# Reciprocal denominators spread by DMA in float32 in place of products with a selector

## The chip, the cores and the metric

The kernel runs on one core of a Trainium2 chip. The metric is the device time of one execution in microseconds; the figure of a kernel is the median of its runs. The core has a tensor engine (PE, whose weight loads are shown as PEld), VectorE (DVE), ScalarE (ACT), GpSimd (POOL) and SyncE (SP), which here issues every DMA. Each engine works through its own list of instructions in order; semaphores tie the lists together.

## The reference

Linear attention with a feature map is followed by a gated layer with a convolution over three tokens. Eight batches, eight heads, 576 tokens, head dimension 64, 128 features; the layer goes from 512 to 1024 and back. Cut to what is computed:

```python
proj = einsum('bhsd,df->bhsf', x, w_phi)           # x is q, then k
proj = proj - max(abs(proj), axis=-1)
phi = concatenate([exp(proj), exp(-proj)], axis=-1)   # 256 features

kv  = einsum('bhsf,bhsd->bhfd', k_p, v)
z   = sum(k_p, axis=2)
num = einsum('bhsf,bhfd->bhsd', q_p, kv)
den = einsum('bhsf,bhf->bhs', q_p, z)[..., None] + 1e-06
x   = num / den                                     # [B, S, 512], the heads side by side

h    = maximum(x @ w_in, 0)
conv = sum over k of conv_w[k] * h shifted by k - 1 tokens
out  = (h * sigmoid(conv)) @ w_out
```

The part that the change touches is the division. Each token of each head has one denominator, and 64 numerators have to be divided by it.

## The kernel before, in words

**Tiling.** Heads are handled in pairs, and two pairs make a quad; a batch has two quads, so four pairs (p = 0 to 3). The 64 dimensions of the first head of a pair lie on partitions 0 to 63 and those of the second on 64 to 127. A quad's tokens come in five groups. `k_process` loads a group of k and v, projects it and adds to kv; `q_process` loads a group of q, projects it, transposes, takes the exponentials and multiplies with kv. The value matrix has a 65th column of ones, so row 64 of the product `nm` is the denominator, and rows 0 to 63 are the numerators.

**Precision.** Many products work on float32 values split into a rounded part and an exact rest (`split`, L57 to L65), three products for one: with rounded weights and the rounded part, with rounded weights and the rest, with the weights' rest and the rounded part.

**From the products to x.** At the end of `q_process`, ScalarE copies the denominators of a group out of row 64 (L374, tile `dr`), and a DMA (L377) brings them into the tile `den`, 72 partitions by 16 elements. ScalarE copies the numerators of both heads into `num`, 128 partitions by 576 tokens (L379). When a pair is complete, `x_process` runs for it. VectorE adds 1e-6 (L392), takes the reciprocal (L393) and splits it into two parts (L396, recorded at the helper's lines L64 and L65). Four DMAs (L399) lay the parts out in `rr`, four rows (part, head) of 576 tokens. Then, for each half c of 290 tokens, a product with the constant selector `sel_r` (four rows by 128 columns of zeros and ones) sums the two parts and spreads them over the head's 64 partitions (L407, PSUM tile `rb`); VectorE multiplies numerators and `rb` (L409, tile `xf`), and `split` gives `xh` (ScalarE) and `xl` (VectorE), on which the MoE layer's first products work.

**The MoE layer.** `h_part` multiplies `xh` and `xl` of the four pairs with w_in (L432) for a chunk of 288 tokens and one on each side that has one; `conv_process` does the convolution, the sigmoid and the gate; `o_part` multiplies with w_out (L491). There are 16 chunks, two per batch.

**Buffers.** PSUM tiles with the tag "g" share four buffers: the projections of q and k, the transposes, `nm`, and `rb`. `xf` has two buffers, `rr` one, `den` three, `num` four, `xh` and `xl` eight each, which is one batch's worth. A batch's `xh` of half c can thus only be written when the previous batch's products with that half are done.

**The order of work.** The parts are generators. A loop at the end merges them: each yields how long the tensor engine is held ("pe"), how long its next operands take ("wait"), or a condition ("until"). Attention is started ahead of MoE by a rule on what is left of each (`ATT_PE`, `MOE_PE`), and gets a lead in priority (`AHEAD`). A tile framework then orders each engine's instructions by priority and by planned times; the parts of `x_process` that touch the division are traced with high priority. What results is a fixed order for each engine; an instruction whose operand is late holds back all that stand behind it on its engine.

Of the kernel before, what the change touches and what calls it, by code (L numbers as in the profile page):

```python
# [18 lines left out]
P = 128  # L19
NQ = 2            # quads (four heads each) per batch  # L20
TC = 288          # tokens per MoE chunk
HW = TC + 2       # tokens of h computed per MoE chunk (one token of halo, even width)
VW = D + 1
NH = 11           # tiles of h
# the order of work
WINDOW = 13       # chains of attention in flight
LAT = 1.7         # latencies stretched by
TAIL_US = 24      # of the MoE's products, what is left when attention's are done
AHEAD = 300       # instructions by which attention goes before the MoE that it was merged with
# quads whose products are in float32, as long as the tensor engine has time, so that nothing has to be split  # L30
NQ_F32 = 2        # q's projections
NKV_F32 = 2       # the products with kv
# [3 lines left out]
def kernel(  # L36
    ctx: ExitStack,
    tc: tile.TileContext,
    qT: bass.AP,     # [B, NQ, 128 = (i, d), 2*S], the last 64 tokens of either pair in the middle
    kT: bass.AP,     # likewise  # L40
    vt: bass.AP,     # [B, NQ, 128, 20*65]
    wbd: bass.AP,    # [128, 256] block diagonal of w_phi
    w_in: bass.AP,   # [8 = (4 c, 2 halves), 128, 512], in float64 twice as many words
    conv_w: bass.AP,  # [128, (8, 3)], likewise
    w_out: bass.AP,  # [8, 128, DM], likewise
    ident: bass.AP,  # [128, 128]
    selr: bass.AP,   # [4, 128]
    out: bass.AP,    # [B, 4, 128, S]
# [8 lines left out]
    def split(src, hi, lo, eng_hi, eng_lo):  # L57
        """hi: src rounded to 12 significant bits, lo: the exact rest."""
        if eng_hi is nc.scalar:
            nc.scalar.activation(out=hi, in_=src, func=AF.Copy)  # L60
        elif eng_hi is nc.gpsimd:
            nc.gpsimd.tensor_scalar(out=hi, in0=src, scalar1=1.0, scalar2=0.0, op0=ALU.mult, op1=ALU.add)  # L62
        else:
            nc.vector.tensor_copy(out=hi, in_=src)  # L64
        eng_lo.tensor_tensor(out=lo, in0=src, in1=hi.bitcast(F32), op=ALU.subtract)  # L65

# [13 lines left out]
    selr_f = sb.tile([4, P], F32, name="selr_f", tag="qr", bufs=2)  # L80
    nc.sync.dma_start(out=selr_f, in_=selr)
    sel_r = cp.tile([4, P], F32R, name="sel_r")
    nc.vector.tensor_copy(out=sel_r, in_=selr_f)

    # Weights that come as float64 arrive as raw 64-bit words, of a high half (sign, 11 bits
    # of exponent, 20 of fraction) and a low half (32 of fraction). The engines build
    #   power = +-2^e   and   w = (1.fraction) * power, rounded to float32 once.
    # Exponents below float32's give zero, those above it infinity or NaN.
# [18 lines left out]
    def weight_split(src, n, hi, lo):  # L107
        """src: [128, 512] weights in DRAM (float32, or the words of float64)."""
        name = f"w{n}_"
        if src.dtype == F32:  # L110
            raw = sb.tile([P, 512], F32, name=f"{name}r", tag="gh", bufs=2)
            nc.sync.dma_start(out=raw, in_=src)
            split(raw, hi, lo, nc.gpsimd, nc.gpsimd)
            return
        raw = sb.tile([P, 1024], I32, name=f"{name}r", tag="gh", bufs=2)
        nc.sync.dma_start(out=raw, in_=src)
        tmp = sb.tile([P, 2, 512], F32, name=f"{name}t", tag="gl", bufs=2)
        w = tmp[:, 0, :]
        float64_round(raw, w, tmp[:, 1, :])
        split(w, hi, lo, nc.scalar, nc.gpsimd)  # L120
# [24 lines left out]
    # The parts below are processes: generators that trace some instructions and then  # L145
    # yield how long the tensor engine is held by them (pe), how long it is until the
    # next part has its operands (wait), or a condition that has to hold (until). The
    # loop at the end merges them into one order in which products of one process
    # cover the latencies of the others.
# [3 lines left out]
    def pe(ns):  # L153
        return ("pe", ns)
# [11 lines left out]
    # A quad is two pairs of heads. Its tokens come in groups: group 0 is the last 64  # L166
    # tokens of both pairs, groups 1 to 4 are 256 tokens of a pair. A tile of 128 tokens
    # holds a pair of heads, one above the other, against block diagonal weights.
# [16 lines left out]
    def project(n, hi, lo, b, qd, g, kind):  # L185
        """The projection of n tiles of two heads less its greatest magnitude per token and head."""
        if b == 0 and kind == "k":
            # the MoE doesn't use its banks yet
            ps = pm.tile([P, n * 256], F32, name=f"{kind}p{b}_{qd}_{g}", tag="m")
        else:  # L190
            ps = pg.tile([P, n * 256], F32, name=f"{kind}p{b}_{qd}_{g}", tag="g", bufs=4)
# [17 lines left out]
    def after(ins, trace):  # L209
        """Trace an instruction that its engine issues behind ins."""  # L210
        if ins is None:
            return trace()
        with tc.issue_after(ins.ins):
            return trace()
# [5 lines left out]
    def k_process(b, qd, g):  # L220
# [39 lines left out]
        if j < 5:  # L260
            for _ in products():
                pass
            yield pe(860 * n)
        else:
            # five groups later in the order than the queries with whose products these alternate:
            # the loads of either's weights hide behind the other's products
            kvgen[j] = products()
            set_ready(("ke", j))
            yield until(("kvd", j))
        if g == 4:  # L270
            # these take the place of the same quad's of the batch before
# [28 lines left out]
    def q_process(b, qd, g):  # L300
# [15 lines left out]
        # in the order (head, tile) the tokens of a head lie side by side  # L316
# [16 lines left out]
        # pairs of heads in this group, each with its tokens' place in the tile and in the sequence  # L333
# [33 lines left out]
        for pr_, o, s0, w in parts:  # L367
            if (b, qd, pr_) not in den:
# [3 lines left out]
            # denominators in the order (16 tokens, head)  # L372
# [3 lines left out]
                                 func=AF.Copy)  # L376
# [7 lines left out]
    def x_process(b, p):  # L384
# [5 lines left out]
        with tc.high_priority():  # L390
            rc = sb.tile([72, 16], F32, name=f"rc{b}_{p}", tag="rc", bufs=2)
            nc.vector.tensor_scalar(out=dn, in0=dn, scalar1=1e-6, scalar2=None, op0=ALU.add)  # L392
            nc.vector.reciprocal(out=rc, in_=dn)  # L393
            rr = sb.tile([4, S], F32R, name=f"rr{b}_{p}", tag="rr", bufs=1)
            rhl = [sb.tile([72, 16], F32R, name=f"rc{j}{b}_{p}", tag=f"rc{j}", bufs=2) for j in range(2)]
            split(rc, rhl[0], rhl[1], nc.vector, nc.vector)  # L396
            for j in range(2):
                for i in range(2):
                    nc.sync.dma_start(out=rr[2 * j + i : 2 * j + i + 1, :].bitcast(F32).rearrange("o (r c) -> o r c", c=16),  # L399
                                      in_=rhl[j].bitcast(F32).rearrange("(r i) c -> i r c", i=2)[i])  # L400
        yield ("wait", 4500)
        for c in range(2):
            yield until(("h", 2 * (b - 1) + c) if b > 0 else None)
            t0 = 0 if c == 0 else S - HW
            with tc.high_priority():
                rb = pg.tile([P, HW], F32, name=f"rb{b}_{p}_{c}", tag="g", bufs=4)
                nc.tensor.matmul(out=rb, lhsT=sel_r, rhs=rr[:, t0 : t0 + HW], start=True, stop=True)  # L407
                xf = sb.tile([P, HW], F32, name=f"xf{b}_{p}_{c}", tag="xf", bufs=2)
                nc.vector.tensor_tensor(out=xf, in0=nt[:, t0 : t0 + HW], in1=rb, op=ALU.mult)  # L409
                xh[b, p, c] = sb.tile([P, HW], F32R, name=f"xh{b}_{p}_{c}", tag="xh", bufs=8)  # L410
                xl[b, p, c] = sb.tile([P, HW], F32R, name=f"xl{b}_{p}_{c}", tag="xl", bufs=8)
                split(xf, xh[b, p, c], xl[b, p, c], nc.scalar, nc.vector)
            set_ready(("x", b, p, c), 2500)
            yield pe(125)

# [28 lines left out]
    def conv_process(n):  # L444
        c = n % 2
        o = 0 if c == 0 else HW - TC
        for f in range(8):
# [6 lines left out]
            # the tap beyond the batch's first and last token falls on nothing  # L454
# [67 lines left out]
    active = []    # [time, process, is a chain, lead in priority], attention's chains and what they spawn  # L522
# [6 lines left out]
    ATT_PE = B * (18 * 330 + 72 * 215 + 18 * 550 + 8 * 6 * 270 + 4 * 250)  # L529
# [6 lines left out]
    def step(p, kind):  # L536
        """Run process p up to its next pause; False when it ended."""
# [23 lines left out]
    while moe is not None or chains or active:  # L561
        while chains and sum(1 for p in active if p[2]) < WINDOW:
            b, x, g, kind = chains.pop(0)
            # the first batch's attention goes before all else
# [22 lines left out]
        else:  # L587
            # nothing is ready: on to the next time at which something is
# [57 lines left out]
```

## Time and profile before

| | |
|---|---|
| median of three runs | 849.68 us (848.51 to 853.46) |
| the profiled execution, first to last instruction | 848.8 us |
| mean granted clock of the tensor engine | 0.981 |
| instructions | 18003 |
| busy: PE, VectorE, ScalarE, GpSimd | 96%, 73%, 67%, 36% |
| products with the selector (L407) | 64 |
| DMAs from `rc` to `rr` (L399) | 128, of 2.2 KB each |
| mean DMA traffic | 58 GB/s |

The profiled execution's span leaves out what lies before its first and after its last instruction; the median is 0.9 us longer. Matmuls are pipelined, so the busy times of single ones overlap, and what one costs is read from the distances of the starts around it. A group's row gives engine, operation, output and inputs, shape and count, then the busy time in us and the mean of one in ns, then the idle time of the engine just before and what ended it.

### The profile page before, as it was taken

The numbers are of one execution on the slowest core, as the hardware profiler recorded it, in microseconds if no ns is written. First come the engines' busy times: TensorE is split into PE (matmuls) and PEld (weight loads), VectorE is DVE, ScalarE is ACT, GpSimd is POOL, SyncE is SP. The second block draws the span as 40 slices with busy tenths as digits, with TensorE's granted clock in tenths as the row PEclk, the third lists the DMA queues.
The fourth block names the chain that finished last, engine by engine and source line by source line (L and its number), as shares of the span: only waits on it lengthen the run. The fifth ranks groups of instructions, "written<-read, shape, count | busy, mean of one in ns | idle before, by whom it ended". The sixth has DMA issues, their size and how long they took to land.

```text
span 848.8 us, 18003 instructions
## 1 busy us (share of the span) xinstructions
PE 817.7 (96%) x6414; PEld 788.2 (93%) x6414; DVE 623.3 (73%) x1327; ACT 571.9 (67%) x1228; POOL 304.0 (36%) x466
## 2 busy tenths in 40 slices
PE   7888879999999999999999999999999999999998
PEld 6867778989999999999999999999999999999998
DVE  5679999898877767776777776777687776756561
ACT  4677787787768667676777867577575876644332
POOL 4557668542442423423142332324144121211110
PEclk9799889999999999999999999999999999999999
DMA  6354331111212212112111211121121100000001
GB/s 194 112 153 125 103 118 51 49 43 53 65 41 65 60 31 68 40 55 56 49 54 47 61 35 57 46 59 54 31 68 36 48 15 22 10 29 29 22 15 49
DMA packets 56336, 49.19 MB, mean 58 GB/s; under 512 B 15028, under 2 KB 54200, under 8 KB 56248
## 3 DMA queue, kind: packets, MB, share of 16 engines
q1 hardware_dynamic: 56248, 48.05, 19.6%
q8 instruction: 51, 0.84, 0.4%
q14 instruction: 37, 0.30, 0.1%
HBM read 38.14 MB, written 9.44 MB: 56 GB/s over the span
## 4 chain that ended last, share of the span: by engine, by line
PE 80%; DVE 9%; ACT 4%; DMA 3%; issue 2%; POOL 0%; SPq 0%; DVEq 0%; POOLq 0%; ACTq 0%
PE op L491 24%; PE hp L432 22%; PE nm L356 8%; PE kv L255 8%; PE tp L320 3%; PE rb L407 2%; PE nm L348 2%; PE qp L199 2%; PE qp L200 2%; PE kp L199 2%; PE qp L201 2%; PE kp L200 2%; PE kp L201 1%; PE kv L251 1%; DMA den<-dr 1%
## 5 line engine op out<-in xcount | busy, mean ns | idle before, releaser
L460 DVE SCALAR_TENSOR_TENSOR c<-h,cw,c 128x288 f32<-128x288 f32 (+1 forms) x256 | 138.6, 550 | 38.4 <-POOL c L455 36.6
L255 PE MATMUL kv<-v,ke 128*128 128x65 f32 x1024 | 161.6, 256 | 0.0
L255 PEld LDWEIGHTS kv<-v,ke 128*128 128x128 f32 x1024 | 156.6, 196 | 4.3 <-issue 1.2
L432 PE MATMUL hp<-xh,win_hi 128*128 128x290 f32 x512 | 153.2, 301 | 1.1 <-ACT os L496 0.6
L432 PE MATMUL hp<-xl,win_hi 128*128 128x290 f32 x512 | 153.5, 300 | 0.0
L455 POOL TENSOR_SCALAR c<-h,cw 128x288 f32<-128x288 f32 x128 | 78.2, 612 | 209.3 <-ACT h L439 172.4
L432 PE MATMUL hp<-xh,win_lo 128*128 128x290 f32 x512 | 153.2, 299 | 0.0
L491 PE MATMUL op<-gh,wout_hi 128*128 128x288 f32 x512 | 152.8, 299 | 0.0
L491 PE MATMUL op<-gh,wout_lo 128*128 128x288 f32 x512 | 151.8, 297 | 0.0
L491 PE MATMUL op<-gl,wout_hi 128*128 128x288 f32 x512 | 151.8, 296 | 0.0
L62 POOL TENSOR_SCALAR kxh<-kr 128x256 fp32r<-128x256 f32 (+1 forms) x80 | 38.0, 475 | 225.7 <-PE kp L200 201.3
L65 DVE TENSOR_TENSOR ql<-qe,qh 128x512 fp32r<-128x512 f32 x112 | 80.1, 728 | 28.2 <-ACT qh L60 28.2
L432 PEld LDWEIGHTS hp<-xh,win_hi 128*128 128x128 f32 x512 | 96.7, 189 | 2.9 <-ACT os L496 1.4
L432 PEld LDWEIGHTS hp<-xh,win_lo 128*128 128x128 f32 x512 | 97.1, 190 | 1.6
L432 PEld LDWEIGHTS hp<-xl,win_hi 128*128 128x128 f32 x512 | 97.0, 189 | 1.0
L491 PEld LDWEIGHTS op<-gh,wout_hi 128*128 128x128 f32 x512 | 96.1, 188 | 0.9
L491 PEld LDWEIGHTS op<-gh,wout_lo 128*128 128x128 f32 x512 | 96.4, 188 | 0.1
L491 PEld LDWEIGHTS op<-gl,wout_hi 128*128 128x128 f32 x512 | 96.2, 188 | 0.2 <-issue 0.2
L439 ACT ACTIVATE h<-hp 128x290 f32<-128x290 f32 x128 | 52.4, 412 | 58.9 <-PE hp L432 56.3
L326 ACT ACTIVATE qe<-tp 128x512 f32<-128x512 f32 x112 | 62.0, 598 | 26.9 <-PE tp L320 22.1
L374 ACT ACTIVATE dr<-nm 1x512 f32<-1x512 f32 (+1 forms) x96 | 46.3, 482 | 48.2 <-PE nm L356 28.2
L204 DVE TENSOR_REDUCE km<-kp 128x4 f32<-128x512 f32 (+1 forms) x80 | 50.4, 631 | 33.8 <-PE kp L201 33.8
(86 smaller groups left out, 2039.1 us busy)
## 6 DMA issues: line engine op xcount, KB each, us to landing
v<-in_vt_dram SPq DMA_DIRECT2D x80, 130.0 KB
out_dram<-os SPq DMA_DIRECT2D x64, 144.0 KB
kr<-in_kT_dram SPq DMA_DIRECT2D x64, 128.0 KB
qr<-in_qT_dram SPq DMA_DIRECT2D x64, 128.0 KB
w_r<-in_w_in_dram SPq DMA_DIRECT2D x8, 512.0 KB
w_r<-in_w_out_dram SPq DMA_DIRECT2D x8, 512.0 KB
rr<-rc SPq DMA_DIRECT2D x128, 2.2 KB
kr<-in_kT_dram SPq DMA_DIRECT2D x16, 64.0 KB
```

The costliest lines, as they stand in the source:

```text
L62: nc.gpsimd.tensor_scalar(out=hi, in0=src, scalar1=1.0, scalar2=0.0, op0=ALU.mult, op1=ALU.add)
L65: eng_lo.tensor_tensor(out=lo, in0=src, in1=hi.bitcast(F32), op=ALU.subtract)
L204: nc.vector.tensor_reduce(out=m, in_=ps3, axis=AX, op=ALU.max, apply_absolute_value=True)
L255: ins = nc.tensor.matmul(out=kp[i][:, s, p0 : p0 + VW], lhsT=lhsT, rhs=v[:, (2 * t + i) * VW : (2 * t + i + 1) * VW], start=False, stop=(g ...
L326: nc.scalar.activation(out=e, in_=tp.rearrange("p i t s -> p i (t s)"), func=AF.Exp, scale=1.0 - 2.0 * s)
L356: ins = after(ins, lambda: nc.tensor.matmul(out=ps[:, i, o : o + w], lhsT=w_, rhs=x_, start=(k == 0), stop=(k == 5)))
L374: nc.scalar.activation(out=dro.rearrange("o (r i c) -> o i r c", i=2, c=16), in_=ps[D : D + 1, :, o : o + w].rearrange("o i (r c) -> o i r ...
L432: nc.tensor.matmul(out=ps, lhsT=w_, rhs=x_, start=(k == 0), stop=(k == 11))
L439: nc.scalar.activation(out=hs, in_=ps, func=AF.Relu)
L455: nc.gpsimd.tensor_scalar(out=cv, in0=hs[:, o : o + TC], scalar1=cw[:, f, 1:2], scalar2=0.0, op0=ALU.mult, op1=ALU.add)
L460: nc.vector.scalar_tensor_tensor(out=cv[:, lo:hi], in0=hs[:, o + j - 1 + lo : o + j - 1 + hi], scalar=cw[:, f, j : j + 1], in1=cv[:, lo:hi ...
L491: nc.tensor.matmul(out=ps, lhsT=w_, rhs=x_, start=(k == 0), stop=(k == 23))
```

## The change

The denominators get their 1e-6 while ScalarE copies them (L374, as a bias). The reciprocal isn't split. Two DMAs in place of four lay it out in `rr`, now two rows of 576 float32. Two further DMAs copy each row to 64 partitions of a new tile `bc`, 128 by 576, with one buffer; their source names the same row 64 times. VectorE multiplies the whole of `num` with `bc` in place, once per pair, and the split reads halves of `num`. The products with the selector, `rb`, `xf`, `sel_r` and its load are gone. The waits that the planning loop is told change (7000 and 1500 ns, and 1200 in place of 2500 for the readiness of x), and `ATT_PE` loses the products' share.

```diff
-    selr_f = sb.tile([4, P], F32, name="selr_f", tag="qr", bufs=2)
-    nc.sync.dma_start(out=selr_f, in_=selr)
-    sel_r = cp.tile([4, P], F32R, name="sel_r")
-    nc.vector.tensor_copy(out=sel_r, in_=selr_f)
...
             nc.scalar.activation(out=dro.rearrange("o (r i c) -> o i r c", i=2, c=16),
                                  in_=ps[D : D + 1, :, o : o + w].rearrange("o i (r c) -> o i r c", c=16),
-                                 func=AF.Copy)
+                                 func=AF.Copy, bias=1e-6)
...
             rc = sb.tile([72, 16], F32, name=f"rc{b}_{p}", tag="rc", bufs=2)
-            nc.vector.tensor_scalar(out=dn, in0=dn, scalar1=1e-6, scalar2=None, op0=ALU.add)
             nc.vector.reciprocal(out=rc, in_=dn)
-            rr = sb.tile([4, S], F32R, name=f"rr{b}_{p}", tag="rr", bufs=1)
-            rhl = [sb.tile([72, 16], F32R, name=f"rc{j}{b}_{p}", tag=f"rc{j}", bufs=2) for j in range(2)]
-            split(rc, rhl[0], rhl[1], nc.vector, nc.vector)
-            for j in range(2):
-                for i in range(2):
-                    nc.sync.dma_start(out=rr[2 * j + i : 2 * j + i + 1, :].bitcast(F32).rearrange("o (r c) -> o r c", c=16),
-                                      in_=rhl[j].bitcast(F32).rearrange("(r i) c -> i r c", i=2)[i])
-        yield ("wait", 4500)
+            rr = sb.tile([2, S], F32, name=f"rr{b}_{p}", tag="rr", bufs=1)
+            bc = sb.tile([P, S], F32, name=f"bc{b}_{p}", tag="bc", bufs=1)
+            for i in range(2):
+                nc.sync.dma_start(out=rr[i : i + 1, :].rearrange("o (r c) -> o r c", c=16),
+                                  in_=rc.rearrange("(r i) c -> i r c", i=2)[i])
+            for i in range(2):
+
+                nc.sync.dma_start(out=bc[D * i : D * i + D, :],
+                                  in_=rr[i : i + 1, :].unsqueeze(1).broadcast_to([1, D, S]))
+        yield ("wait", 7000)
+        with tc.high_priority():
+            nc.vector.tensor_tensor(out=nt, in0=nt, in1=bc, op=ALU.mult)
+        yield ("wait", 1500)
         for c in range(2):
             yield until(("h", 2 * (b - 1) + c) if b > 0 else None)
             t0 = 0 if c == 0 else S - HW
             with tc.high_priority():
-                rb = pg.tile([P, HW], F32, name=f"rb{b}_{p}_{c}", tag="g", bufs=4)
-                nc.tensor.matmul(out=rb, lhsT=sel_r, rhs=rr[:, t0 : t0 + HW], start=True, stop=True)
-                xf = sb.tile([P, HW], F32, name=f"xf{b}_{p}_{c}", tag="xf", bufs=2)
-                nc.vector.tensor_tensor(out=xf, in0=nt[:, t0 : t0 + HW], in1=rb, op=ALU.mult)
                 xh[b, p, c] = sb.tile([P, HW], F32R, name=f"xh{b}_{p}_{c}", tag="xh", bufs=8)
                 xl[b, p, c] = sb.tile([P, HW], F32R, name=f"xl{b}_{p}_{c}", tag="xl", bufs=8)
-                split(xf, xh[b, p, c], xl[b, p, c], nc.scalar, nc.vector)
-            set_ready(("x", b, p, c), 2500)
-            yield pe(125)
+                split(nt[:, t0 : t0 + HW], xh[b, p, c], xl[b, p, c], nc.scalar, nc.vector)
+            set_ready(("x", b, p, c), 1200)
+            yield ("wait", 100)
...
-    ATT_PE = B * (18 * 330 + 72 * 215 + 18 * 550 + 8 * 6 * 270 + 4 * 250)
+    ATT_PE = B * (18 * 330 + 72 * 215 + 18 * 550 + 8 * 6 * 270)
```

## The prediction, made before the changed kernel ran

> **What bounds the kernel now.** I first read the page's busy shares and its chain of waits:
>
> ```profile
> span 848.8 us, 18003 instructions
> ...
> PE 817.7 (96%) x6414; PEld 788.2 (93%) x6414; DVE 623.3 (73%) x1327; ACT 571.9 (67%) x1228; POOL 304.0 (36%) x466
> ...
> q1 hardware_dynamic: 56248, 48.05, 19.6%
> ...
> PE 80%; DVE 9%; ACT 4%; DMA 3%; issue 2%; POOL 0%; SPq 0%; DVEq 0%; POOLq 0%; ACTq 0%
> PE op L491 24%; PE hp L432 22%; PE nm L356 8%; PE kv L255 8%; PE tp L320 3%; PE rb L407 2%; PE nm L348 2%; PE qp L199 2%; PE qp L200 2%; PE kp L199 2%; PE qp L201 2%; PE kp L200 2%; PE kp L201 1%; PE kv L251 1%; DMA den<-dr 1%
> ```
>
> TensorE sets the end, and the products to be removed (L407) are on the chain. An average hides stages, so next the busy time by stretches (us of PE, PEld, DVE, ACT, POOL; clock; DMA share; GB/s):
>
> ```profile
> 85.00:160.00 75.00, 65.81 (x500) 61.96 (x499) 72.23 (x132) 58.68 (x128) 52.04 (x61) 0.91 0.29 84
> ...
> 480.00:560.00 80.00, 79.53 (x645) 77.89 (x644) 59.06 (x132) 53.67 (x116) 28.36 (x48) 1.00 0.17 47
> 560.00:640.00 80.00, 79.77 (x660) 77.80 (x660) 56.98 (x127) 56.43 (x125) 23.67 (x43) 1.00 0.19 54
> 640.00:720.00 80.00, 79.56 (x642) 77.27 (x641) 57.98 (x129) 57.12 (x122) 21.17 (x34) 1.00 0.10 29
> ...
> 825.00:849.00 24.00, 20.43 (x154) 20.20 (x152) 5.48 (x15) 5.66 (x15) 0.00 (x0) 0.97 0.15 50
> ```
>
> There are three stages. Up to about 160 us VectorE is the bound (72.2 of 75). From 160 to about 745, where attention ends, PE is full and VectorE has slack: 59.06+56.98+57.98 = 174.0 of 240 us, 72.5%. Behind that there are almost only MoE products. The beat of the middle stage is read from three long pieces of the chain in order of time, which recur once per batch:
>
> ```profile
> 480.31 1.61 PE hp L432 x12
> ...
> 580.13 1.61 PE hp L432 x12
> ...
> 679.80 1.61 PE hp L432 x12
> ```
>
> That is 99.7 us per batch of four pairs of heads, 24.9 us per pair. VectorE works 0.725 x 24.9 = 18.05 us of it.
>
> **The removed products.** A busy time says little here, since matmuls overlap. In order of time on PE:
>
> ```profile
> 586.32 0.30 PE L432 MATMUL hp<-xh,win_hi 128*128 128x290 f32 x1
> 586.46 0.30 PE L432 MATMUL hp<-xl,win_hi 128*128 128x290 f32 x1
> 586.68 0.40 PE L407 MATMUL rb<-rr,sel_r 4*128 4x290 f32 x1
> 587.01 0.41 PE L432 MATMUL hp<-xh,win_lo 128*128 128x290 f32 x1
> 587.25 0.30 PE L432 MATMUL hp<-xh,win_hi 128*128 128x290 f32 x1
> ```
>
> Products of this stream start about 0.135 us apart. From 586.46 to 587.25 are 0.79 us; without rb the two steps would take 0.27. One rb thus costs 0.52 us, more than its columns, since the product behind it is late too. Two per pair: 1.04 us, so the PE needs 23.9 us per pair. With 28 pairs behind the first batch and 0.5 us for each of 56 products, up to 28 us are to be had, if nothing takes PE's place. The other side effect, one user fewer of the four PSUM buffers "g", is taken at nothing: PE hardly waits in this stage.
>
> **VectorE and ScalarE.** The groups by form:
>
> ```profile
> L407 PE MATMUL rb<-rr,sel_r 4*128 4x290 f32 x64 | 24.1, 387 | 4.7 <-DVE ks L206 4.6
> L409 DVE TENSOR_TENSOR xf<-num,rb 128x290 f32<-128x290 f32 x64 | 28.0, 447 | 2.8 <-PE rb L407 2.8
> L392 DVE TENSOR_SCALAR den<-den 72x16 f32<-72x16 f32 x32 | 7.7, 242 | 29.4 <-DMA den<-dr 26.2 <-DMA v<-in_vt_dram 2.2 <-issue 0.9
> L64 DVE CAST rc<-rc 72x16 fp32r<-72x16 f32 x32 | 7.4, 230 | 0.3
> L65 DVE TENSOR_TENSOR rc<-rc,rc 72x16 fp32r<-72x16 f32 x32 | 8.4, 263 | 0.4
> L65 DVE TENSOR_TENSOR ql<-qe,qh 128x512 fp32r<-128x512 f32 x112 | 80.1, 728 | 28.2 <-ACT qh L60 28.2
> L65 DVE TENSOR_TENSOR gl<-c,gh 128x288 fp32r<-128x288 f32 x128 | 51.4, 457 | 24.3 <-ACT gh L60 24.2
> ```
>
> Three small operations go: 7.7+7.4+8.4 = 23.5 us. Two multiplications of 290 columns (894 ns) become one of 576 with both inputs in SBUF. No row has that width; from ql and gl a column costs (728-457)/(512-288) = 1.21 ns, so 728+64x1.21 = 805 ns. Its bounds are 728 ns (ql, which is narrower) and 914 (two of gl). Together VectorE saves 23.5/32+0.09 = 0.8 us per pair and would work 17.25. The addition of 1e-6 goes into L374, which runs anyway: nothing on ScalarE. The splits are as before.
>
> **The new transfers.** rr has two DMAs per pair in place of four, and two new ones follow, each copying one row of 576 float32 from one partition to 64 partitions: 64 pieces of 2304 bytes. The rows that price them:
>
> ```profile
> L399 SPq DMA_DIRECT2D rr<-rc x128: 707/728/1305, 50.1 to 741.3; - x128
> ...
> L497 SPq DMA_DIRECT2D out_dram<-os x64: 332/343/587, 199.6 to 846.0; - x64
> ```
>
> ```profile
> 401.45 0.58 SPq L377 DMA_DIRECT2D den<-dr  x1
> ```
>
> ```profile
> 404.60 0.17 DVE L392 TENSOR_SCALAR den<-den 72x16 f32<-72x16 f32 x1 [1.03 <-DMA den<-dr]
> ```
>
> Issues on SP: four of 0.73 become two of 0.73 and two of between 0.34 and 0.73, no more than before. But the new pair has to wait on SP until rr has landed, and loads of k, q, v and stores of the output queue behind it. A small transfer lands 404.60-402.03 = 2.57 us after its issue ended. Before, one such hop stood between the reciprocal and its use; now there are two, plus the time in which 2 x 147,456 bytes move.
>
> That time is what the trace doesn't show: no transfer of before takes much out of a single partition. Low end: all 16 DMA engines at the rate of the last stretch (only stores, rows of 1152 bytes): 50/(16x0.15) = 20.8 bytes per ns and engine, 111 ns per piece, four pieces each, 0.45 us per copy. High end: the pieces follow one another, because all come out of the same partition: 64x111 ns = 7.1 us. Between them: by q1 a mean packet has 48.05 MB/56248 = 854 bytes and takes 0.196x16x848.8/56248 = 47.3 ns; one of 1152 takes 55.4; the slope is 37 bytes per ns. If the packets' fixed parts overlap and only bytes queue, 64x2304/37 = 4.0 us. I take 5.5, the middle of 4.0 and 7.1, 11.0 per pair: I hold the serial case for likelier, because 64 readings of one partition share a source, while every quick row above spreads over many.
>
> The Trainium skill, "SBUF — State Buffer", Door 1: The DMA port swizzle, says the same from its own figures: partitions share 16 DMA ports, eight to a port, and it measured 27.6 GB/s for a tile on partitions 0 to 3. Both rows of rr are on such a port, so 147,456 bytes at 27.2 GB/s per port make an estimate of 5.4 us per copy and 10.8 for the pair. No run here shows it yet; the sum with it would be 943, 5 us below mine.
>
> **The wait.** From the reciprocal's end to the multiplication: 2x0.73 (issue rr) + 2.57 + 0.34 (first copy's issue; the second's is covered) + 11.0 + 2.57 = 17.9 us. The diff's plan allows 7.0 (yield of 7000). VectorE works in order, so it meets the difference, 10.9 us, as a stall at the multiplication; behind it queue ks, qs, ql, the convolution and gl, and PE waits for each of them. What such a stall costs PE is seen once, as VectorE's and PE's rows in order of time:
>
> ```profile
> 540.71 0.17 DVE L392 TENSOR_SCALAR den<-den 72x16 f32<-72x16 f32 x1 [3.52 <-DMA den<-dr]
> ```
>
> ```profile
> 543.12 0.37 PE L407 MATMUL rb<-rr,sel_r 4*128 4x290 f32 x1 [0.47 <-DVE ks L206]
> ```
>
> Of 3.5 us PE lost 0.5, so PE's lead covers about 3. A stall of 10.9 isn't covered. VectorE becomes the bound of the middle stage: 17.25+10.9 = 28.15 us per pair against 24.9, +3.25. From 160 to 745 are 585/24.9 = 23.5 pairs: +76 us. In the first stage, where VectorE has no slack, I count two pairs (two of the first four fall behind 85 us): +22. The last batch's pairs are covered by MoE products. Sum: 848.8+76+22 = 947 for the span, 948 with the 0.9 us by which the median 849.7 exceeds it. With copies of 7.1 us the stall is 14.1, the pair 31.35: 848.8+152+28+0.9 = 1030. With 4.0 us it is 7.9: 25.15, +6+16, 872. The forecast's own range is 870 to 1020; idle gaps of PE might also lower its clock, as in the first stage (0.91).
>
> **The rivals.** (1) *The copies are spread and quick.* Then the wait is 17.9-11.0+0.9 = 7.8 us, a stall of 0.8, which PE's lead of 3 covers; PE stays the bound and 28 us come off, two more in the first stage: 848.8+0.9-30 = 820. For it: the 19.6% DMA share, and that 64 pieces divide evenly. Against it: the single source. The Trainium skill, "DMA: Bandwidth & Descriptors", How many engines (k), lets a copy whose slowest dimension is 64 run on 16 engines, which bears on the number of engines and not on the source.
> (2) *Loads, not VectorE, become late.* The copies occupy all engines for 11 us per pair, and loads issued behind them wait. POOL shows how early k's loads are:
>
> ```profile
> POOL kxh L62 <- PE kp L200: 201.3, 48, 13.6
> ```
>
> On average 201.3/48 = 4.2 us early, so 6.8 us of 11 would reach PE: 23.9+6.8 = 30.7 per pair, +5.8x23.5 = +136, 986. Against it: one group of loads per pair at most meets a copy, and many loads are issued long before.
> (3) *Serial, but hidden.* VectorE comes to the multiplication late enough for most of the wait to be over; a stall of 6 leaves 23.25, below PE's 23.9, but each then costs PE 6-3 = 3 against 1 gained: between 849.7-28 = 822 and 849.7+2x23.5 = 897, 859 in the middle. For it: the multiplication could be placed behind other work; against it: it has high priority, and is put where its operand is planned to be ready.
>
> **How the numbers follow.** Forecast 0.47; rival 1 0.36; rival 2 0.08; rival 3 0.09 (a third each way). About 0.5% is what a measurement of this kernel can tell from no change. Faster: 0.36+0.03 = 0.39; same 0.03; slower 0.47+0.08+0.03 = 0.58. The predicted time is the forecast's, 948. As cases of both signs are heavy, the range reaches from below rival 1 (815) to 1020.
>
> **What will show it.** Right: a large idle time of VectorE ahead of its 128x576 multiplication, released by the DMA bc<-rr, some 11 us each; VectorE's busy and idle share at this line filling the span; PE below 90% from 160 to 745; the DMA share in that stage risen by 11/28. Wrong: a wait of a microsecond or two there, hp products without gaps where rb stood and 24 us per pair. Rival 2 would show POOL waiting for DMA kr or qr. The step on which all hangs is the rate out of one partition; next is the lead of about 3 us, read from one stall.

## The result, and the profile after

The changed kernel takes 1089.95 us (median of four runs, 1088.83 to 1092.1) against 850.33 us for the kernel before, a ratio of 1.282 with a 95% interval of 1.279 to 1.285. It is slower, as forecast, but by 240 us and not by 98, and outside the range that ended at 1020. One of the ten executions of experiment 10 below took 4306.58 us and is left out of that experiment's ratio.

The first lines of the page of the changed kernel, then its DMA queue and its chain of waits:

```profile
span 1090.3 us, 17595 instructions
...
PE 865.4 (79%) x6350; PEld 842.7 (77%) x6350; DVE 608.1 (56%) x1198; ACT 570.1 (52%) x1228; POOL 300.3 (28%) x466
...
q1 hardware_dynamic: 58288, 57.34, 41.9%
...
DMA bc<-rr 13%; PE op L487 8%; PE hp L428 5%; DVE c L456 2%; DMA rr<-rc 2%; DMA den<-dr 1%; PE nm L352 1%; PE kv L251 1%; DVE num L400 1%; SPq L175 1%; PE tp L316 1%; ACT gh L60 1%; DVE qm L200 1%; DVE xl L65 1%; SPq L396 1%
```

The 64 products are gone, and yet PE is busy for 865.4 us in place of 817.7: on average its instructions take longer. It is idle for 1090.3-865.4 = 224.9 us in place of 31.1. The copies are the largest item of the chain, which could be followed back over half of the span (its shares add up to 50%), and the DMA engines are busy for 41.9% in place of 19.6%, with 9.3 MB more moved. From the list of who waited for whom (us in all, times, longest):

```profile
DVE num L400 <- DMA bc<-rr: 296.7, 31, 12.4
...
ACT dr L370 <- DMA den<-dr: 106.4, 14, 11.7
...
POOL kxh L62 <- DMA kr<-in_kT_dram: 25.9, 7, 8.9
```

VectorE waited 297 us at the new multiplication, in 31 of 32 pairs, 9.6 us each. In order of time on VectorE, then on PE, and a piece of the chain:

```profile
517.53 0.76 DVE L400 TENSOR_TENSOR num<-num,bc 128x576 f32<-128x576 f32 x1 [8.89 <-DMA bc<-rr]
```

```profile
520.49 0.61 PE L428 MATMUL hp<-xh,win_hi 128*128 128x290 f32 x1 [6.35 <-ACT h L435]
```

```profile
572.45 11.87 DMA bc<-rr
```

VectorE stands still for 8.89 us, and PE behind it for 6.35. The chain's piece of 11.87 us runs from the copies' issue to the multiplication. In the trace's packet records the 128 pieces of a pair take 11.0 us from the first start to the last end (median of 32 pairs), 294,912 bytes/11.0 us = 26.8 GB/s, and one piece holds its engine for 1251 ns (median). The stretches of 0 to 160 us, the middle and the end:

```profile
0.00:160.00 160.00, 112.84 (x730) 101.36 (x731) 105.40 (x176) 96.32 (x204) 83.51 (x106) 0.83 0.60 114
160.00:960.00 800.00, 640.91 (x4824) 631.19 (x4823) 443.44 (x889) 429.93 (x931) 201.95 (x333) 0.88 0.43 46
960.00:1090.00 130.00, 111.62 (x800) 110.20 (x798) 59.23 (x133) 43.88 (x95) 14.87 (x27) 0.95 0.19 28
```

PE fills 80% of the middle (640.91 of 800) where it had filled 99%, and its granted clock there is 0.88 in place of 1.00. VectorE, which I had expected to be the bound, is busy for 55% of the middle (443.44 of 800). It waits 253.2 us of the middle at the multiplication (26 times) and stands idle for another 103 us there. The first reciprocals of batches 3 and 7 start at 377 and 897 us: 32.5 us per pair, where 28.15 had been forecast.

### The profile page after: what moved, and what is told of

Read it like the earlier page. It is cut to its first block, busy times and chain, and to the rows that moved or that the text cites. A ratio compares the mean times of both kernels' runs of the same rounds, so it can differ in the third digit from the quotient of the medians.

```text
span 1090.3 us, 17595 instructions
## 1 busy us (share of the span) xinstructions
PE 865.4 (79%) x6350; PEld 842.7 (77%) x6350; DVE 608.1 (56%) x1198; ACT 570.1 (52%) x1228; POOL 300.3 (28%) x466
## 3 DMA queue, kind: packets, MB, share of 16 engines
q1 hardware_dynamic: 58288, 57.34, 41.9%
## 4 chain that ended last, share of the span: by engine, by line
PE 18%; DMA 16%; DVE 7%; ACT 4%; issue 3%; SPq 2%; POOL 0%; DVEq 0%; ACTq 0%; POOLq 0%
DMA bc<-rr 13%; PE op L487 8%; PE hp L428 5%; DVE c L456 2%; DMA rr<-rc 2%; DMA den<-dr 1%; PE nm L352 1%; PE kv L251 1%; DVE num L400 1%; SPq L175 1%; PE tp L316 1%; ACT gh L60 1%; DVE qm L200 1%; DVE xl L65 1%; SPq L396 1%
## 5 line engine op out<-in xcount | busy, mean ns | idle before, releaser
L428 PE MATMUL hp<-xh,win_hi 128*128 128x290 f32 x512 | 162.0, 318 | 40.6 <-ACT h L435 21.6
L400 DVE TENSOR_TENSOR num<-num,bc 128x576 f32<-128x576 f32 x32 | 24.3, 759 | 302.4 <-DMA bc<-rr 296.7
L487 PE MATMUL op<-gh,wout_hi 128*128 128x288 f32 x512 | 163.4, 319 | 25.3 <-ACT os L492 24.5
L487 PE MATMUL op<-gl,wout_hi 128*128 128x288 f32 x512 | 161.9, 316 | 0.0
L487 PE MATMUL op<-gh,wout_lo 128*128 128x288 f32 x512 | 161.1, 315 | 0.0
L428 PEld LDWEIGHTS hp<-xh,win_hi 128*128 128x128 f32 x512 | 104.2, 204 | 43.0 <-ACT h L435 22.3
L487 PEld LDWEIGHTS op<-gh,wout_hi 128*128 128x128 f32 x512 | 105.9, 207 | 27.0 <-ACT os L492 25.6
L370 ACT ACTIVATE dr<-nm 1x512 f32<-1x512 f32 (+1 forms) x96 | 46.2, 482 | 133.5 <-DMA den<-dr 106.4
L487 PEld LDWEIGHTS op<-gl,wout_hi 128*128 128x128 f32 x512 | 106.0, 207 | 0.0
L487 PEld LDWEIGHTS op<-gh,wout_lo 128*128 128x128 f32 x512 | 105.6, 206 | 0.0
L316 PE MATMUL tp<-idn,qs 128*128 128x128 f32 x288 | 67.8, 307 | 45.6 <-DVE qs L202 44.0
```

The source lines that it names most:

```text
L316: nc.tensor.transpose(out=tp[:, i, t, :], in_=pr[:, 2 * t + i, :], identity=idn)
L370: nc.scalar.activation(out=dro.rearrange("o (r i c) -> o i r c", i=2, c=16), in_=ps[D : D + 1, :, o : o + w].rearrange("o i (r c) -> o i r ...
L400: nc.vector.tensor_tensor(out=nt, in0=nt, in1=bc, op=ALU.mult)
L428: nc.tensor.matmul(out=ps, lhsT=w_, rhs=x_, start=(k == 0), stop=(k == 11))
L487: nc.tensor.matmul(out=ps, lhsT=w_, rhs=x_, start=(k == 0), stop=(k == 23))
```

## The experiments

Theory A: all pieces leave one place in SBUF, one behind another; what waits for them, or stands behind them, holds the kernel. Its rivals: B, the volume into 64 partitions or the DMA engines; C, the new order and the longer chain. Kernels 1 to 9 start from the changed one (3 has the multiplication of 2), 10 and 11 from that of experiment 1.

**1. The same copies out of DRAM.**

```diff
-            rr = sb.tile([2, S], F32, name=f"rr{b}_{p}", tag="rr", bufs=1)
+            rr = dp.tile([2, S], F32, name=f"rr{b}_{p}", tag="rr", bufs=2)    # dp: a pool in DRAM
...
                 nc.sync.dma_start(out=bc[D * i : D * i + D, :],
-                                  in_=rr[i : i + 1, :].unsqueeze(1).broadcast_to([1, D, S]))
+                                  in_=rr[i : i + 1, :].broadcast_to([D, S]))
```

> The reciprocals are laid out in DRAM and not in two rows of SBUF; the two copies to 64 partitions per pair read the same row 64 times from there. Pieces, bytes, targets, queue and the order of VectorE's instructions from the first batch on are those of the changed kernel. Theory A (the pieces leave one SBUF partition one after another, 294,912 bytes in 11.0 us per pair, and VectorE waits in order): the copies become quick, VectorE waits below 2.5 us per pair in place of 9.6, the time is between 815 and 860 us. Theory B (it is the volume of 128 pieces into 64 partitions, or the DMA engines themselves, however read): the copies still take about 11 us, the time stays within 3% of 1090. Theory C (the changed order and the longer chain of two transfers, whatever their speed): VectorE's wait falls but the time stays above 950.

Measured: 840.5 us, ratio 0.987 (0.984 to 0.990). Its page, and its wait at the multiplication:

```profile
PE 790.1 (94%) x6350; PEld 774.3 (92%) x6350; DVE 619.7 (74%) x1198; ACT 571.6 (68%) x1228; POOL 318.9 (38%) x466
...
q1 hardware_dynamic: 58288, 57.34, 23.0%
```

```profile
DVE num L400 <- DMA bc<-rr: 43.8, 23, 3.7
```

The same number of packets and bytes as in the changed kernel, into the same partitions, occupies 23.0% and not 41.9%; a piece takes 93 ns in place of 1251 (medians), the pair 2.0 us in place of 11.0. Theories B and C fall: with another source the same order of work is 250 us quicker, and quicker than the kernel before.

**2. Sixteen tokens copied.**

```diff
-                                  in_=rr[i : i + 1, :].unsqueeze(1).broadcast_to([1, D, S]))
+                                  in_=rr[i : i + 1, 0:16].unsqueeze(1).broadcast_to([1, D, 16]))
...
-            nc.vector.tensor_tensor(out=nt, in0=nt, in1=bc, op=ALU.mult)
+            nv = nt.rearrange("p (r c) -> p r c", c=16)
+            nc.vector.tensor_tensor(out=nv, in0=nv, in1=bc.unsqueeze(1).broadcast_to([P, S // 16, 16]), op=ALU.mult)
```

> The copies have 16 tokens in place of 576 (64 pieces of 64 bytes each), and the multiplication uses these 16 reciprocals for all tokens: the right denominators are left out, all other work stays. Theory A and B: with the bytes gone, VectorE's wait at the multiplication falls below 2 us per pair, PE is full again from 160 us on, the time is 812 to 835. Theory C: it stays above 950.

Measured: 835.9 us, ratio 0.983 (0.980 to 0.985), a microsecond above the expected span of times. This is what the rest of the change is worth when copies cost next to nothing. Its page, its stretches and its wait:

```profile
span 835.2 us, 17593 instructions
...
PE 793.2 (95%) x6350; PEld 777.0 (93%) x6350; DVE 615.7 (74%) x1198; ACT 570.5 (68%) x1228; POOL 324.8 (39%) x466
```

```profile
0.00:160.00 160.00, 128.94 (x916) 116.39 (x917) 131.43 (x219) 113.01 (x243) 101.97 (x124) 0.93 0.40 116
160.00:720.00 560.00, 553.37 (x4616) 550.92 (x4616) 423.44 (x844) 412.83 (x888) 206.55 (x313) 0.99 0.19 49
```

```profile
DVE num L400 <- DMA bc<-rr: 33.6, 22, 4.8
```

The first stretch of the kernel before:

```profile
0.00:160.00 160.00, 136.49 (x955) 124.30 (x955) 134.09 (x246) 114.89 (x246) 100.68 (x125) 0.90 0.40 117
```

PE's busy time falls by 817.7-793.2 = 24.5 us with the products. Its idle time rises from 31.1 to 42.0, and 7.6 of these 10.9 us come before 160 us (160-128.94 against 160-136.49); what sets that stretch wasn't tried. VectorE still waits 33.6 us at the multiplication, though nearly nothing is moved: by elimination that is the latency of the second transfer, which experiments 10 and 11 come back to.

**3. The full copies, read by nobody.** Beside the small copies of experiment 2 (into a tile `bt`, ahead of them in the program's text), the full ones are issued.

```diff
+            bt = sb.tile([P, 16], F32, name=f"bt{b}_{p}", tag="bt", bufs=1)
+            for i in range(2):
+                nc.sync.dma_start(out=bt[D * i : D * i + D, :],
+                                  in_=rr[i : i + 1, 0:16].unsqueeze(1).broadcast_to([1, D, 16]))
```

> As with 16 tokens, but the two full copies out of one partition are issued too, behind the small ones, and nobody reads them: the DMA engines are held as long as in the changed kernel, VectorE doesn't wait for it. Right denominators are left out. Theory A1 (the loss is VectorE's wait in order): 820 to 870 us. Theory A2 (the loss is what queues behind the copies in the DMA engines: loads, denominators, stores): above 950, with waits for kr, qr, den or out in place of bc.

Measured: 1011.9 us, ratio 1.189 (1.187 to 1.192). The waits for DMAs:

```profile
DVE num L405 <- DMA bt<-rr: 123.9, 29, 7.7
...
ACT dr L370 <- DMA den<-dr: 101.6, 13, 13.2
...
DVE rc L388 <- DMA den<-dr: 45.6, 11, 7.0
```

Without any reader the copies cost 176 us over experiment 2: a large part of the loss needs nobody who reads them, as A2 says. The denominators' transfers are late: ScalarE cannot overwrite the one row `dr` until its transfer has been read, and waits up to 13.2 us. But the experiment doesn't take VectorE's wait away, as it was meant to. SyncE's order and the multiplication of one pair:

```profile
470.60 0.55 SPq L396 DMA_DIRECT2D bt<-rr  x1
471.21 0.59 SPq L400 DMA_DIRECT2D bc<-rr  x1
471.90 0.52 SPq L396 DMA_DIRECT2D bt<-rr  x1
```

```profile
479.51 0.76 DVE L405 TENSOR_TENSOR num<-num,bt 128x576 f32<-128x576 f32 x1 [4.94 <-DMA bt<-rr]
```

In 18 of the 32 pairs the second small copy was issued behind the first full one, and VectorE then waits 5.7 us on average (103 of the 123.9 us); in the other 14 it waits 1.5 us. So the 176 us hold a wait in VectorE's order too, and how much of them is the queue alone isn't known.

**4. The multiplication later in VectorE's order.**

```diff
-        yield ("wait", 7000)
-        with tc.high_priority():
-            nc.vector.tensor_tensor(out=nt, in0=nt, in1=bc, op=ALU.mult)
+        yield ("wait", 20000)
+        after(last[0], lambda: nc.vector.tensor_tensor(out=nt, in0=nt, in1=bc, op=ALU.mult))
```

`last` holds the subtraction of the projection traced last.

> Everything computed as in the changed kernel, with the same slow copies; the multiplication is told to follow the last projection that was traced 20 us later in the plan, so it stands some 50 instructions later in VectorE's order. Theory A1 (the copies are planned as quick, so VectorE arrives too early): VectorE's wait for bc falls from 297 us to below 100, and the time to 850 to 950. Theory A2 (queues behind the copies) or C: the time stays above 1000.

Measured: 1031.8 us, ratio 1.213 (1.209 to 1.216). Its waits:

```profile
DVE num L401 <- DMA bc<-rr: 104.6, 11, 11.6
...
DVE rc L390 <- DMA den<-dr: 74.2, 12, 11.6
ACT dr L372 <- DMA den<-dr: 53.9, 10, 11.6
```

VectorE's wait for bc falls to a third, and only 58 us are won. The two waits for the denominators come to 128 us in place of 116 in the changed kernel, and the time stays above 1000, as A2 and C had it. That these waits make the rest is the likelier reading; what the later x costs PE was not measured by itself here.

**5 and 6. Four rows in one DMA port, four rows in four ports.** Both lay each row out four times and copy 16 pieces from each; only the partitions differ.

```diff
-            rr = sb.tile([2, S], F32, name=f"rr{b}_{p}", tag="rr", bufs=1)
+            rr = sb.tile([36, S], F32, name=f"rr{b}_{p}", tag="rr", bufs=1)          # experiment 5
+            rv = [rr[32 * i : 32 * i + 4, :] for i in range(2)]
+            rr = sb.tile([16, S], F32, name=f"rr{b}_{p}", tag="rr", bufs=1)          # experiment 6
+            rv = [rr.rearrange("(a g) s -> g a s", g=4)[i] for i in range(2)]
...
+                for a in range(4):
+                    nc.sync.dma_start(out=rv[i][a : a + 1, :].rearrange("o (r c) -> o r c", c=16),
+                                      in_=rc.rearrange("(r i) c -> i r c", i=2)[i])
...
-                                  in_=rr[i : i + 1, :].unsqueeze(1).broadcast_to([1, D, S]))
+                                  in_=rv[i].unsqueeze(1).broadcast_to([4, D // 4, S]))
```

> Each reciprocal row is laid out four times, on partitions 0 to 3 for the first head of a pair and 32 to 35 for the second (eight small DMAs in place of two); a copy then takes 16 pieces from each of four partitions. By the Trainium skill, "SBUF — State Buffer", Door 1: The DMA port swizzle, these eight partitions share one DMA port. Theory P (the port is the limit): the two copies still take 11 us per pair, the time stays above 1050. Theory S (a single partition is the limit): four sources are read at once, the copies take under 4 us per pair, the time falls below 950.

> The same eight small DMAs and the same shape of copy, but the four rows of a head lie on partitions 0, 4, 8 and 12 (1, 5, 9 and 13 for the second head), which by the same section are four ports. Theory P and theory S alike: the copies take 3 to 4 us per pair, the time falls to between 850 and 950. If neither holds and the number of pieces or DMA engines decides, 11 us or more and above 1050 here too.

Measured: 1149.6 us (ratio 1.350, 1.344 to 1.356) and 888.0 us (1.043, 1.038 to 1.047). Lines of the page, a piece of the chain and waits, first of experiment 5, then of experiment 6:

```profile
span 1148.3 us, 17733 instructions
...
PE 866.1 (75%) x6350; PEld 843.6 (73%) x6350; DVE 609.8 (53%) x1198; ACT 569.8 (50%) x1228; POOL 303.6 (26%) x466
...
q1 hardware_dynamic: 66736, 57.78, 22.3%
```

```profile
509.90 12.12 DMA bc<-rr
```

```profile
DVE num L401 <- DMA bc<-rr: 348.5, 32, 13.8
...
ACT dr L370 <- DMA den<-dr: 105.1, 13, 13.6
```

```profile
span 886.6 us, 17733 instructions
...
PE 807.3 (91%) x6350; PEld 784.8 (89%) x6350; DVE 617.7 (70%) x1198; ACT 569.6 (64%) x1228; POOL 314.9 (36%) x466
```

```profile
529.48 4.20 DMA bc<-rr
```

```profile
DVE num L401 <- DMA bc<-rr: 92.5, 28, 5.7
```

In the packet records the two copies take 12.1 us (experiment 5) and 3.7 us (experiment 6). Four neighbouring source rows are no quicker than one; four rows that lie four partitions apart, with the same pieces and the same shape of copy, are three times as quick. What neighbouring partitions share is the limit, and theory S falls. Experiment 5 lies 60 us above the changed kernel, more than 32 x 1.1 us of copying: eight issues in place of two now stand ahead of the copies (SPq L394 is 7% of its chain). The Trainium skill, "SBUF — State Buffer", Door 1: The DMA port swizzle, puts partitions 0 to 3 and 32 to 35 on one port and measured 27.6 GB/s for one. The 26.8 GB/s here, for reading out of SBUF, agree with it. That 32 to 35 share the limit with 0 to 3 isn't shown: in experiment 5 the second copy's first piece starts 5.9 us behind the first copy's, when that copy is all but over (6.2 us), so the two follow one another anyway.

**7. Half of the tokens copied.** As experiment 2, with 288 in place of 16.

> The copies hold 288 of 576 tokens (64 pieces of 1152 bytes each), and the multiplication uses them for both halves: the second half's denominators are left out. Theory A: the transfers take 5.5 us per pair and VectorE waits 4 to 5 us at the multiplication. If PE's lead of about 3 us that I read from one stall is right, the time is 850 to 900; if every microsecond of a held queue costs as much as in the changed kernel (254 us above the kernel with 16 tokens for 11 us per pair), it is 836+127 = 963.

Measured: 920.4 us, ratio 1.081 (1.074 to 1.088), between the two expectations. Its page, a piece of its chain, and its wait:

```profile
span 920.5 us, 17594 instructions
...
PE 821.6 (89%) x6350; PEld 800.6 (87%) x6350; DVE 609.4 (66%) x1198; ACT 570.8 (62%) x1228; POOL 312.8 (34%) x466
```

```profile
586.87 6.56 DMA bc<-rr
```

```profile
DVE num L400 <- DMA bc<-rr: 138.0, 32, 7.9
```

Half the bytes take 11.87-6.56 = 5.3 us less. VectorE waits 4.3 us per pair and PE's idle time is (98.9-42.0)/32 = 1.8 us per pair above experiment 2's. The price of a wait is not proportional: over experiment 2, the first half of the transfer costs 84 us and the second half 170.

**8. The copies issued by GpSimd.**

```diff
-                nc.sync.dma_start(out=bc[D * i : D * i + D, :],
+                nc.gpsimd.dma_start(out=bc[D * i : D * i + D, :],
```

> As the changed kernel, but the two slow copies are issued by GpSimd and not by SyncE, so that the small transfers of denominators, the loads and the stores no longer stand behind them in one queue. Copies, multiplication and VectorE's wait in order remain. If the queue is the larger part of the loss, as the kernel with copies that nobody reads says (1012 of 1090), ScalarE's wait for den (106 us) vanishes and the time falls below 1000; if the DMA engines themselves are held whoever issues, it stays within 3% of 1090.

Measured: 1081.3 us, ratio 1.270 (1.263 to 1.277). Queues and waits:

```profile
q0 software_dynamic: 3072, 9.44, 28.8%
q1 hardware_dynamic: 53168, 47.89, 14.7%
```

```profile
DVE num L400 <- DMA bc<-rr: 272.8, 32, 11.2
...
ACT dr L370 <- DMA den<-dr: 68.7, 11, 10.1
```

The copies have a queue of their own and still hold others up: ScalarE waits up to 10.1 us for the denominators. The time stays within 3% of 1090, so it isn't SyncE's queue alone; the pair of copies takes 11.0 us here too, and the engines are held whoever issues. GpSimd itself now stands still before these issues, 46.9 us in all until rr has landed, so what leaving SyncE's queue is worth isn't known.

**9. Two buffers for the row of denominators**, paid for with one of h.

```diff
-NH = 11
+NH = 10
...
-        dr = sb.tile([P, 2 * n * P], F32, name=f"dr{b}_{qd}_{g}", tag="dr", bufs=1)
+        dr = sb.tile([P, 2 * n * P], F32, name=f"dr{b}_{qd}_{g}", tag="dr", bufs=2)
```

> The changed kernel with two buffers of the row of denominators in place of one, so that ScalarE need not wait until a small transfer that stands behind the slow copies has read the last row; one buffer of h fewer pays for the space (ten in place of eleven), which can only cost time. If ScalarE's wait for den (106 us in the changed kernel) is a loss of its own, the time falls below 1050 and that wait below 40 us; if VectorE's wait at the multiplication and the other transfers behind the copies set the time anyway, it stays between 1060 and 1110 though ScalarE's wait is gone.

Measured: 1081.9 us, ratio 1.273 (1.266 to 1.280). ScalarE's wait for den is gone from the list of waits, and the longest are:

```profile
DVE num L400 <- DMA bc<-rr: 312.0, 32, 13.9
...
ACT ke L232 <- DVE ks L202: 163.5, 32, 20.6
```

The second expectation holds: with the one wait removed others grow, VectorE's from 296.7 to 312.0 us and this one of ScalarE's from 87.2 to 163.5. What the missing buffer of h costs wasn't measured apart.

**10 and 11. A version that beats both.** With the rows in DRAM, one store in place of two and two buffers of bc; then also the multiplication later.

```diff
-            bc = sb.tile([P, S], F32, name=f"bc{b}_{p}", tag="bc", bufs=1)
-            for i in range(2):
-                nc.sync.dma_start(out=rr[i : i + 1, :].rearrange("o (r c) -> (o r) c", c=16),
-                                  in_=rc.rearrange("(r i) c -> i r c", i=2)[i])
+            bc = sb.tile([P, S], F32, name=f"bc{b}_{p}", tag="bc", bufs=2)
+            nc.sync.dma_start(out=rr.rearrange("i (r c) -> r i c", c=16), in_=rc)
...
-        yield ("wait", 7000)                                                         # experiment 11
-        with tc.high_priority():
-            nc.vector.tensor_tensor(out=nt, in0=nt, in1=bc, op=ALU.mult)
+        yield ("wait", 9000)
+        after(last[0], lambda: nc.vector.tensor_tensor(out=nt, in0=nt, in1=bc, op=ALU.mult))
```

> The kernel with the rows in DRAM, with one store of the reciprocals per pair in place of two and two buffers of the spread reciprocals in place of one (the SBUF that the rows held is free). If SyncE's issues (0.7 us each) and the single buffer are what is left of VectorE's wait (44 us in that kernel), the wait falls below 30 us and the time to 832 to 838; if it is the two hops' latency, the time stays within 0.5% of 840.

> As the one before, and the multiplication is told to follow the last projection traced 9 us later in the plan, so VectorE comes to it later. If the hops' latency, met by VectorE in order, is what keeps the gain at 10 us and not at the 28 us that the removed products cost PE, the wait falls below 10 us and the time to 825 to 835. If the later x costs PE as much as the wait did, the time is 838 or more.

Measured: 841.7 us (ratio 0.990, 0.988 to 0.993) and 834.4 us (0.980, 0.976 to 0.984). The wait of experiment 10, then of experiment 11, and the latter's page:

```profile
DVE num L398 <- DMA bc<-rr: 41.5, 22, 4.8
```

```profile
DVE num L399 <- DMA bc<-rr: 4.3, 2, 3.9
```

```profile
span 833.5 us, 17595 instructions
...
PE 796.4 (96%) x6350; PEld 782.8 (94%) x6350; DVE 609.8 (73%) x1198; ACT 572.2 (69%) x1228; POOL 307.1 (37%) x466
```

Fewer issues and a second buffer do nothing that shows (841.7 against 840.5); what is left, by elimination, is the latency of two hops. Placing the multiplication behind it takes the wait away, and the kernel is 2% quicker than the one before. PE's idle time, 37.1 us, is still 6 above that of before.

## Why the prediction was right or wrong

**Right: the direction, the slow copies as its cause, and VectorE's wait in order.** "11.0 per pair" was measured at 11.0 in the packet records; its reason, a shared source, is shown by experiments 1, 5 and 6. That the number fits so well is in part luck: 5.5 per copy was the middle of 4.0 and 7.1, and neither of the two readings gives it. The stall of "10.9 us" is 9.6 on average. The multiplication, "805 ns", takes 758 (median), inside its bounds. Removing the products was priced at "up to 28 us" of PE's time; 24.5 of busy time were measured. That 14 remain as time in experiment 2 (849.7 to 835.9) is rival 1's sum of 820 missed by 16: it took the second hop for covered by PE's lead, and counted 2 us of gain in the first stage, where 7.6 of idle time were added.

**Wrong: "VectorE becomes the bound of the middle stage: 17.25+10.9 = 28.15 us per pair against 24.9, +3.25".** This is the step that failed. It takes VectorE to be at work or at that one wait all the time; in fact it was idle elsewhere for 103 us of the middle, and a pair took 32.5 us. And it lets PE make up, between two stalls, for what it lost in one. PE cannot: its own work fills nearly all of a pair's time. Its period is its work plus the stall less the lead. That is the formula that I used for rival 3 ("each then costs PE 6-3 = 3 against 1 gained") and not for the forecast. With my own numbers it gives 23.9+(10.9-3) = 31.8 us per pair, 6.9 above 24.9, 162 us in place of 76 over 23.5 pairs, and a sum of 848.8+0.9+162+22 = 1034, beyond the end of the range, as the sum with slower copies (1030) had been. With the 9.6 us of wait that were measured it gives 30.5 per pair, and with the clock below, 72.2/32 = 2.3, it gives 32.8 against 32.5. PE's idle time per pair above experiment 2's, against VectorE's mean wait per pair at the multiplication:

| kernel | VectorE's wait, us | PE's idle, us | PE's busy time above 793.2, us |
|---|---|---|---|
| experiment 1 (DRAM) | 1.4 | 0.3 | -3.1 |
| experiment 6 (four ports) | 2.9 | 1.2 | 14.1 |
| experiment 7 (half) | 4.3 | 1.8 | 28.4 |
| changed kernel | 9.3 | 5.7 | 72.2 |
| experiment 5 (one port) | 10.9 | 7.5 | 72.9 |
| experiment 3 (read by nobody) | 3.9 | 3.9 | 48.8 |
| experiment 4 (multiplication later) | 3.3 | 4.6 | 50.3 |

(Sums of the waits, and idle time above 42.0 us, each over 32 pairs. In experiments 3 and 4 the spans are 1010.3 and 1031.4 us and PE is busy for 842.0 and 843.5.) In the first five rows the multiplication stands at its place and differs only in what it waits for: behind some 3 us, most of each further microsecond reaches PE (3.9 us of 5.0 from experiment 7 to the changed kernel). The last two rows don't lie on that line. There PE loses as much as VectorE waits at the multiplication, or more, though the copies are as slow as in the changed kernel. So the formula comes near the time, but VectorE's one wait isn't all that stands behind it: what else the copies hold up reaches PE too, and the forecast's sum had nothing for it.

**Left out of the sum: the clock.** "Idle gaps of PE might also lower its clock" had no price. In the changed kernel and in experiment 2 PE has the same 6350 instructions, 865.4 us against 793.2: 72.2 us, with 0.88 against 0.99 granted in the middle. The whole difference between the two kernels, 1090.3-835.2 = 255.1 us, is these 72.2 and 224.9-42.0 = 182.9 of idle time. No run set the clock alone, but the trace settles it. In its clock records the granted share is either 1.00 or 0.50. A gap of PE, and two stretches behind it:

```profile
753.57 1.08 PE L316 MATMUL tp<-idn,qs 128*128 128x128 f32 x4 [9.39 <-DVE qs L202]
```

```profile
753.60:758.80 5.20, 5.20 (x25) 5.19 (x25) 3.28 (x7) 3.78 (x10) 0.00 (x0) 0.50 0.10 33
758.80:764.00 5.20, 5.20 (x48) 5.20 (x47) 4.15 (x8) 2.74 (x6) 3.00 (x4) 1.00 0.16 46
```

PE is busy all through both, with 25 instructions in 5.2 us at 0.50 and 48 at 1.00. Of PE's busy time 175.3 us lie in stretches of half clock in the changed kernel and 27.4 in experiment 2; half of the difference, 74.0 us, is what the lower clock costs, and 72.2 are to be explained. The Trainium skill, "TensorE: Matmul & The Clock Gate", HAM oscillation — how this bites in real kernels, warns of idle gaps of PE above some 3.4 us, behind which it runs at half clock for a while. The trace agrees: in the changed kernel PE has 30 gaps above 3.4 us (up to 9.4), each with half clock from 1.9 to 5.1 us after its start, and in the kernel before and in experiment 2 it has none. But shorter gaps bring half clock too: ten times behind 160 us in experiment 7, beside gaps of 1.8 to 3.0 us.

**The rivals.** Rival 1 (quick copies) fell with the 11.0 us. Rival 2 was taken for an alternative with chance 0.08, but both happen: the transfers behind the copies are late as well (experiment 3), though it is the small ones of the denominators more than k's loads, for which GpSimd waited 25.9 us in the changed kernel. They don't simply add up, as experiment 9 shows. Rival 3 (hidden) would have needed the multiplication elsewhere; experiment 4 put it there and won 58 us; the other transfers were as late as before.

How the 255 us divide between VectorE's own wait and what stands behind the copies can't be given as a sum: experiment 3 has 176 with 123.9 us of VectorE's wait still in it, experiment 4 has 196 left with a third of the wait at the multiplication. This stays open.

## What to carry to other kernels

A DMA that reads one SBUF row many times is bound by its one source, here at 26.8 GB/s, however many engines take part, and it holds the engines for everything behind it; bring the row to DRAM first, or lay it out over partitions that lie four apart. Price a stall of a helper engine by what the full engine loses, its own work plus the stall less its lead, and not by the helper's busy time; look for what else the slow transfer holds up, since moving its reader or dropping it left 176 to 196 of 254 us here; then add what a lower clock costs the full engine once its gaps are some microseconds long (72 us here). When products are replaced by a transfer, place the reader behind the latency in its engine's order, or the wait eats a part of what the products gave (7 us between experiments 10 and 11, of PE's 24.5). When an experiment orders transfers, read from the trace in which order they were issued.

## What the runs showed of the hardware that was not expected

Pieces that wait for a busy source occupy their DMA engines all the while: 1251 ns each against 93 ns from DRAM. Transfers on another queue are held too (experiment 8). Experiment 5, with the engines busy for only 22.3% in its page's queue row, holds the denominators as long as the changed kernel does (105.1 us of ScalarE's wait against 106.4). Reading the same row of DRAM 64 times is quick, 2.0 us for two copies of 147,456 bytes each. PE's granted clock is 1.00 or 0.50, and 0.50 came beside gaps of 1.8 to 3.0 us as well (experiment 7).
